# Stores and reloads issued by another engine, late products over all 128 rows, and element-wise work exchanged between ScalarE, VectorE and GpSimd, in a memory attention and two-MLP kernel

## The chip, the cores and the metric

The program runs on one core of a Trainium2 chip. The metric is the device time of one execution in microseconds, median of the runs. On the core TensorE multiplies (in the rows: PE, and PEld for its weight loads), VectorE (DVE), ScalarE (ACT) and GpSimd (POOL) work element-wise, and each engine runs its own instructions strictly in the order written, waiting on semaphores for the others. Transfers run on 16 DMA engines; an instruction on some engine's queue issues them. In the kernel before, all transfers are issued by SyncE (SP, in the rows SPq).

## The reference

```python
# attention between x (8,8,512,64) and state (8,8,32,64), both ways
scores = scale * x @ state.T          # per batch and head: (512, 32)
xread  = softmax(scores) @ state      # every token reads the memory
scores2 = scale * state @ x.T         # (32, 512)
sread  = softmax(scores2) @ x         # every memory slot reads the tokens
t = concat([xread, sread], axis=2)    # 8 x 544 rows of 512
# first MLP
h = t @ w_in                          # 512 -> 2048
y = (relu(h) ** 2) @ w_out            # 2048 -> 512
# second MLP, with a softmax gate and a layer norm
h2 = y @ w2_in                        # 512 -> 1024
s = h2 * softmax(h2)
out = (layer_norm(s) * g_ln) @ w2_out # 1024 -> 512
```

The weights come as 64-bit floats. All products are float32 in quality: an operand is split into a high part, rounded to what TensorE reads in one pass (float32r), and a low part, the rest; a product is three matmuls, high by high, high by low and low by high (`triple`).

## The kernel before, in words

The xread product is folded into the first MLP: since xread is softmax times state, the kernel makes state times w_in once per batch ("sw", 128 rows of head and slot per group of heads, 2048 columns) and multiplies the softmax with it. So a token's hidden layer needs 2 groups of 128 rows in place of 4.

**Prologue.** The 64-bit words of w_in come in 16 units of 128x512 (`fetch_pair`, `fetch_w1in`), are converted by some five VectorE and two ScalarE operations (`convert_parts`), stored for later (`w1i_d`, L213), and multiplied with the state of batches 0 to 3 (`sw_part`). The result goes through ScalarE into a buffer and is stored to HBM (`sw_d`, L287 and L289). Eight units are done ahead of the main loop, together with attention of batch 0.

**Main loop**, 144 steps. An item is a pair (block b, slice f of 128 hidden columns); the first 32 items are the 16 slices of blocks 0 and 1, by halves, and each block after that has 16 items in a row; block 8 holds the sread rows of all batches (256 columns in place of 512). In a step, `hidden` makes 128x512 of the hidden layer in PSUM (6 matmuls, 12 in block 8), ScalarE takes its relu into SBUF (L544), and it is squared by ScalarE (first 16 steps, L546) or by VectorE (after that, L548, r times r). One step later `high` casts it on VectorE (L553) and `low` subtracts on VectorE (L558); two steps later `project` multiplies with w_out into four accumulators (12 matmuls).

Every four steps a chunk of sw is reloaded with four transfers (`load_sw`, L355 for batches 0 to 3), three steps before its first use, and a step later split by `split_sw`: high on ScalarE (L107), low on GpSimd (L108), two tiles of 128x512 each. The buffers of these reloads (tag "stg", four) are those of the weight fetches also.

Between them run, a few pieces a step, attention of the next batch (`attention`), the conversion of the other weights, and in steps 32 to 63 the state-times-w_in products of batches 4 to 7 (`late_part`): 32 times, one product of 128 rows with the high part of the state (L340: rows 0 to 63 are the high part of w_in, rows 64 to 127 its low part, the state stands twice), and one with the low part of the state over rows 0 to 63 (L341).

`sread` (two halves per batch) multiplies softmax and tokens with a stationary tile of 64 columns; the two heads of a pair, i = 0 and 1, go to PSUM rows 0 to 63 and 64 to 127, four token groups t for the one head and then four for the other.

After the loop comes the second MLP, 34 tiles of 128 rows, which the change doesn't touch. Pools set when a buffer is free; the framework orders each engine's queue, in part by its own estimate of durations, so that the order in the trace isn't the program's order line by line.

Of the kernel before, what the change touches and what calls it, by code (L numbers as in the profile page):

```python
# [8 lines left out]
F32 = mybir.dt.float32  # L9
# [3 lines left out]
AF = mybir.ActivationFunctionType  # L13
ALU = mybir.AluOpType
# [6 lines left out]
def memory_attention_relu2_solu(  # L21
# [15 lines left out]
    nc = tc.nc  # L37
    P = 128
    B, H, S, D = x.shape
# [5 lines left out]
    NT = S // P  # L45
    NHP = H // 2
    NQ = H // 4
    NF = F1 // P
    NM = DM // P
    FC = 512  # L50
# [6 lines left out]
    sw_d = [dram.tile([P, B // 4, F1], F32, name=f"sw_d{hp}", tag=f"sw{hp}") for hp in range(NHP)]  # L57
    sw2_d = dram.tile([P, H, F1], F32, name="sw2_d", tag="sw2")

    w1i_d = [dram.tile([P, 2, F1], F32, name=f"w1i_d{k}", tag=f"w1i{k}") for k in range(NM)]  # L60
# [42 lines left out]
    ]  # L103
    sr = srp.tile([P, NHP, NSR], F32, name="sr")

    def split(hi, lo, src, eng=None):
        nc.scalar.activation(out=hi, in_=src, func=AF.Copy)  # L107
        (eng or nc.vector).tensor_tensor(out=lo, in0=src, in1=hi.bitcast(F32), op=ALU.subtract)  # L108

    def triple(ps, pairs, first, last):  # L110

# [6 lines left out]
    def bank(name):  # L118
        return ps_m.tile([P, 512], F32, tag="m", name=name)
# [4 lines left out]
    def u_tile(name):  # L124
        return up_.tile([P, 2, 512], F32R, tag="u", name=name)

    def sw_tile(name):
        return swp.tile([P, 2, 512], F32R, tag="sw", name=name)
# [77 lines left out]
    def convert_w1in(u, st):  # L206

        c, k = divmod(u, NM)

        t = u_tile("w1in")  # L210

        def done():
            nc.sync.dma_start(out=w1i_d[k][:, :, c * FC : (c + 1) * FC], in_=t.bitcast(F32))  # L213
            w1u[u] = t

        flying.append(convert_parts(st, t[:, 0, :], t[:, 1, :], done))
# [55 lines left out]
    def sw_part(u, j):  # L272

        c, hp = divmod(u, NM)
        i = hp % 2
        single = c == 0 and j < 2
        if j % 2 == 0 or single:
            sw_ev[0] = evp.tile([P, 2, 512], F32, tag="ev", name="ev_sw")
        ev = sw_ev[0]
        ps = ps_a.tile([P, 512], F32, tag=f"acc{hp}", name="ps_sw") if u < AHEAD and j < 2 else bank("ps_sw")  # L280
        lh = bd[i][j][:, hp // 2, i].rearrange("p n b -> p (n b)")
        ll = bd[i][j][:, hp // 2, 1 - i].rearrange("p n b -> p (n b)")
        t = w1u[u]
        triple(ps, [(lh, ll, t[:, 0, :], t[:, 1, :])], True, True)
        nc.scalar.activation(out=ev[:, j % 2, :], in_=ps, func=AF.Copy)
        if single:
            nc.sync.dma_start(out=sw_d[hp][:, j, c * FC : (c + 1) * FC], in_=ev[:, j % 2, :])  # L287
        elif j % 2 == 1:
            nc.sync.dma_start(out=sw_d[hp][:, j - 1 : j + 1, c * FC : (c + 1) * FC], in_=ev)  # L289
        if j == 1:  # L290
            w1u.pop(u)

# [37 lines left out]
    def late_part(u, i):  # L330
        c, k = divmod(u, NM)
        if i == 0:
            sw_ev[0] = evp.tile([P, 2, 512], F32, tag="ev", name="ev_sw")
        ev = sw_ev[0]
        ps = bank("ps_sw")
        t = late_w[u]
        h = 2 * k + i
        st = late_st[h // 4]
        o = (h % 4) * P
        nc.tensor.matmul(out=ps, lhsT=st[:, 0, o : o + P], rhs=t[:, i, :], start=True, stop=False)  # L340
        nc.tensor.matmul(out=ps, lhsT=st[:D, 1, o : o + P], rhs=t[:D, i, :], start=False, stop=True)  # L341
        nc.scalar.activation(out=ev[:, i, :], in_=ps, func=AF.Copy)
        if i == 1:
            nc.sync.dma_start(out=sw2_d[:, 2 * k : 2 * k + 2, c * FC : (c + 1) * FC], in_=ev)
            late_w.pop(u)
# [4 lines left out]
    def load_sw(b, c):  # L350
        st = stgp.tile([P, 2, 512], F32, tag="stg", name="stg")
        if b < B // 2:
            for q in range(NQ):
                for i in range(2):
                    nc.sync.dma_start(  # L355
                        out=st[i * 2 * NS : (i + 1) * 2 * NS, q, :],
                        in_=sw_d[2 * q + i][b % 2 :: 2, b // 2, c * FC : (c + 1) * FC],
                    )
        else:
            r = (b - B // 2) * NS  # L360
            for h in range(4):
                nc.sync.dma_start(
                    out=st[h * NS : (h + 1) * NS],
                    in_=sw2_d[r : r + NS, h::4, c * FC : (c + 1) * FC],
                )
        loading[b, c] = st

    def split_sw(b, c):
        st = loading.pop((b, c))
        loaded[b, c] = []  # L370
        for q in range(NQ):
            t = sw_tile("sw")
            split(t[:, 0, :], t[:, 1, :], st[:, q, :], nc.gpsimd)
            loaded[b, c].append(t)

    def load_w1in(c, kk):
# [16 lines left out]
    def attention(b):  # L393
# [82 lines left out]
        def sread(half):  # L476
            if half == 0:
                v["ps_sr"] = bank("ps_sr")
            ps = v["ps_sr"]
            for hp in (2 * half, 2 * half + 1):  # L480
                for i in range(2):
                    h = 2 * hp + i
                    for t in range(NT):
                        nc.tensor.matmul(  # L484
                            out=ps[i * D : (i + 1) * D, hp * NS : (hp + 1) * NS],
                            lhsT=xs_t[b][hp][:, t, i, :],
                            rhs=v["e2", t // 2][:, t % 2, h * NS : (h + 1) * NS],
                            start=(t == 0),
                            stop=(t == NT - 1),
                        )  # L490
            if half == 1:
                nc.scalar.activation(
                    out=sr[:, :, b * NS : (b + 1) * NS],
                    in_=ps[:, : NHP * NS].rearrange("p (h n) -> p h n", n=NS),
                    func=AF.Copy,
                )
# [37 lines left out]
    def hidden(blk, f, w, ah, al, n):  # L534

        c0 = (f % FPC) * P
        ps = ps_h.tile([P, 512], F32, tag="h", name="ps_h")[:, :n]
        pairs = [
            (w[k][:, 0, c0 : c0 + P], w[k][:, 1, c0 : c0 + P], ah[:, k, :], al[:, k, :])
            for k in range(ah.shape[1])  # L540
        ]
        triple(ps, pairs, True, True)
        r = rp.tile([P, 512], F32, tag="r", name="r")[:, :n]
        nc.scalar.activation(out=r, in_=ps, func=AF.Relu)  # L544
        if len(done) < NF:
            nc.scalar.activation(out=r, in_=r, func=AF.Square)  # L546
        else:
            nc.vector.tensor_tensor(out=r, in0=r, in1=r, op=ALU.mult)  # L548
        return r

    def high(b, f, n, r):
        gh = gp.tile([P, 512], F32R, tag="gh", name="gh")[:, :n]
        nc.vector.tensor_copy(out=gh, in_=r)  # L553
        return b, f, n, r, gh

    def low(b, f, n, r, gh):
# [4 lines left out]
    x2_ev = {}  # L561
# [3 lines left out]
    def project(blk, f, n, gh, gl, m):  # L565
        part = NF // 2 if blk < 2 else NF
        if f % part == 0 and m == 0:
            acc[blk] = [ps_a.tile([P, 512], F32, tag=f"acc{i}", name=f"acc{i}")[:, :n] for i in range(NM)]
        wt = w1o[f // 2]
        o = (f % 2) * 512 + m * P  # L570
        triple(acc[blk][m], [(wt[:, 0, o : o + P], wt[:, 1, o : o + P], gh, gl)], f % part == 0, f % part == part - 1)
        if f % part == part - 1:
            if m % 2 == 0:
                x2_ev[0] = evp.tile([P, 2, 512], F32, tag="ev", name="ev_x2")
            ev = x2_ev[0][:, m % 2, :n]
            if f > part:
                nc.vector.tensor_tensor(out=ev, in0=acc[blk][m], in1=x2_part[blk, m // 2][:, m % 2, :], op=ALU.add)
            elif m % 2 == 0:
                nc.scalar.activation(out=ev, in_=acc[blk][m], func=AF.Copy)
            else:  # L580
                nc.vector.tensor_copy(out=ev, in_=acc[blk][m])
            if m % 2 == 1:
                to = x2p_d[blk] if f + 1 < NF else x2_d[blk]
                nc.sync.dma_start(out=to[:, m - 1 : m + 1, :], in_=x2_ev[0][:, :, :n])


    NU = NM * NC1
# [33 lines left out]
    for u in range(NM):  # L621
        begin("i", u)
        for k in range(5):
            advance()
            if k % 2 == 0 and first:
                for piece in first.pop(0):
                    piece()
        if u > 0:
            sw_part(u - 1, 0)
# [159 lines left out]
    done = []  # L789
    for s, (b, f) in enumerate(items):  # L790
# [7 lines left out]
        if g % 5 == 2 and 0 <= g // 5 + 1 < 16:  # L798
            n = g // 5 + 1
# [27 lines left out]
        h = high(*squares.pop(0)) if squares else None  # L827
# [10 lines left out]
        n = S if b < B else NSR  # L838
# [10 lines left out]
        if b < 2 and f in (NF - 4, NF - 3):  # L849
            i = f - NF + 4  # L850
# [43 lines left out]
    for s in range(1, len(tiles) + 2):  # L894
        if s == 1:
            reload_w2(7, 1)
        if s < len(tiles):
            blk, t = tiles[s]
            i = order.index(blk) + 1
# [7 lines left out]
            ps = up(s, blk, t)  # L907
# [36 lines left out]
```

## Time and profile before

| what | value |
|---|---|
| median of 3 runs | 1171.35 us (1170.88 to 1172.41) |
| the profiled execution | 1172.12 us |
| its span in the profile | 1170.3 us |
| TensorE busy | 1124.8 us, 96% of the span |
| VectorE busy | 746.5 us, 64% |
| ScalarE busy | 484.1 us, 41% |
| GpSimd busy | 143.9 us, 12% |

Busy time is the time in which an instruction of the engine is under way; TensorE's instructions overlap, so that a matmul of 0.39 us can start 0.23 us after the one before it. A clock of 1.00 in the rows is TensorE's full 2.4 GHz, 0.5 is 1.2 GHz. "A <- B" in a row of waits says that A stood idle until B was done.

### The profile page before, as it was taken

What the parts mean: (1) busy time and instruction counts of PE and PEld (TensorE: products, weight loads), DVE (VectorE), ACT (ScalarE), POOL (GpSimd) and SP (SyncE); (2) the same over time, 40 slices, a digit from 0 to 9 for tenths busy, and PEclk for the clock granted to TensorE, in tenths of its full rate; (3) what the DMA queues carried; (4) which work ended last, traced back from release to release, by engine and by line L of the source; (5) the groups of instructions that cost most, each with busy time, mean ns of one, the idle gap of its engine ahead of it and who ended that gap; (6) DMA issues with size and microseconds to landing.
All of it is one profiled execution on the core that took longest, in us unless ns stands there. A gap on an engine that the chain in (4) does not pass through costs nothing.

```text
span 1170.3 us, 15242 instructions
## 1 busy us (share of the span) xinstructions
PE 1124.8 (96%) x5672; PEld 914.3 (78%) x5672; DVE 746.5 (64%) x1357; ACT 484.1 (41%) x845; POOL 143.9 (12%) x122
## 2 busy tenths in 40 slices
PE   4787999999999999999999999999999999999997
PEld 2556778777777778888888889988888888888886
DVE  7869999778557569588585554765545454445442
ACT  4657664345445345244342212443434333334232
POOL 0101302132221122222111110000000000000000
PEclk9788999999999999999999999999999999999999
DMA  8775794567565454331310114621101011000000
GB/s 228 242 231 184 267 286 127 161 184 223 180 180 176 128 165 135 89 119 64 91 37 18 73 54 150 229 82 54 64 19 63 18 63 37 28 18 27 19 26 30
DMA packets 93323, 133.66 MB, mean 114 GB/s; under 512 B 45248, under 2 KB 45760, under 8 KB 93248
## 3 DMA queue, kind: packets, MB, share of 16 engines
q1 hardware_dynamic: 93248, 132.68, 36.5%
q8 instruction: 45, 0.74, 0.3%
q14 instruction: 30, 0.25, 0.1%
HBM read 83.37 MB, written 49.28 MB: 113 GB/s over the span
## 4 chain that ended last, share of the span: by engine, by line
PE 84%; DVE 8%; DMA 3%; ACT 2%; issue 1%; POOL 1%; SPq 0%; POOLq 0%; ACTq 0%; DVEq 0%
PE h L703 15%; PE acc L114 10%; PE acc L115 9%; PE acc L116 9%; PE ps_o L754 5%; PE ps_o L752 5%; PE ps_o L753 5%; PE ps_h L114 5%; PE ps_h L116 5%; PE ps_h L115 5%; PE ps_t L742 2%; PE ps_sr L484 2%; PE ps_sw L341 1%; DMA stg<-sw_d 1%; PE ps_x L400 1%
## 5 line engine op out<-in xcount | busy, mean ns | idle before, releaser
L114 PE MATMUL acc<-gh,w1out 128*128 128x512 f32 (+1 forms) x576 | 223.5, 389 | 5.3 <-DVE gh L553 3.9
L115 PE MATMUL acc<-gl,w1out 128*128 128x512 f32 (+1 forms) x576 | 219.4, 381 | 0.0
L116 PE MATMUL acc<-gh,w1out 128*128 128x512 f32 (+1 forms) x576 | 219.2, 381 | 0.0
L548 DVE TENSOR_TENSOR r<-r 128x512 f32<-128x512 f32 (+1 forms) x128 | 99.5, 778 | 119.4 <-ACT r L544 119.3
L108 POOL TENSOR_TENSOR sw<-stg,sw 128x512 fp32r<-128x512 f32 x64 | 101.0, 1590 | 417.1 <-ACT sw L107 245.3
L703 PE MATMUL h<-w,x2h 128*128 128x512 f32 x544 | 148.6, 395 | 0.0
L544 ACT ACTIVATE r<-ps_h 128x512 f32<-128x512 f32 (+1 forms) x144 | 82.3, 572 | 134.9 <-PE ps_h L116 131.2
L114 PEld LDWEIGHTS acc<-gh,w1out 128*128 128x128 f32 x576 | 109.4, 190 | 34.1 <-issue 7.4
L116 PEld LDWEIGHTS acc<-gh,w1out 128*128 128x128 f32 x576 | 109.3, 190 | 20.7
L115 PEld LDWEIGHTS acc<-gl,w1out 128*128 128x128 f32 x576 | 109.5, 190 | 19.8 <-issue 0.5
L703 PEld LDWEIGHTS h<-w,x2h 128*128 128x128 f32 x544 | 99.7, 188 | 18.9
L114 PE MATMUL ps_h<-ah,sw 128*128 128x512 f32 x256 | 107.7, 421 | 0.9 <-ACT ah L107 0.9
L752 PE MATMUL ps_o<-w,lh 128*128 128x512 f32 x272 | 106.1, 390 | 1.0 <-ACT lh L107 1.0
L754 PE MATMUL ps_o<-w,ll 128*128 128x512 f32 x272 | 106.2, 390 | 0.6 <-DVE ll L108 0.6
L753 PE MATMUL ps_o<-w,lh 128*128 128x512 f32 x272 | 105.9, 389 | 0.0
L116 PE MATMUL ps_h<-ah,sw 128*128 128x512 f32 x256 | 101.9, 398 | 1.4 <-POOL sw L108 1.4
L558 DVE TENSOR_TENSOR gl<-r,gh 128x512 fp32r<-128x512 f32 (+1 forms) x144 | 100.5, 698 | 3.4
L115 PE MATMUL ps_h<-al,sw 128*128 128x512 f32 x256 | 101.0, 394 | 0.0
L721 ACT ACTIVATE e<-h,nm 128x1024 f32<-128x1024 f32 x34 | 38.0, 1116 | 143.7 <-DVE nm L718 143.7
L717 DVE TENSOR_REDUCE nm<-h 128x1 f32<-128x1024 f32 x34 | 41.6, 1224 | 86.1 <-PE h L703 86.1
L553 DVE CAST gh<-r 128x512 fp32r<-128x512 f32 (+1 forms) x144 | 80.6, 560 | 9.8 <-ACT r L546 1.9
L703 PE MATMUL h<-w,x2l 128*128 128x512 f32 x272 | 83.8, 389 | 0.0
(131 smaller groups left out, 1715.9 us busy)
## 6 DMA issues: line engine op xcount, KB each, us to landing
stg<-sw_d SPq DMA_DIRECT2D x128, 128.0 KB, 3.0
sw_d<-ev_sw SPq DMA_DIRECT2D x28, 512.0 KB, 4.1
st<-in_moe_w_out_dram SPq DMA_DIRECT2D x24, 512.0 KB, 4.7
xs<-in_x_dram SPq DMA_DIRECT2D x64, 128.0 KB, 3.2
w1i_d<-w1in SPq DMA_DIRECT2D x16, 512.0 KB, 3.9
st<-in_moe_w_in_dram SPq DMA_DIRECT2D x16, 512.0 KB, 5.3
x_d<-ev_x SPq DMA_DIRECT2D x16, 512.0 KB, 2.7
w1in<-w1i_d SPq DMA_DIRECT2D x32, 256.0 KB, 4.7
```

Of the source, the lines that this page charges most:

```text
L108: (eng or nc.vector).tensor_tensor(out=lo, in0=src, in1=hi.bitcast(F32), op=ALU.subtract)
L114: nc.tensor.matmul(out=ps, lhsT=lh, rhs=rh, start=first and i == 0, stop=False)
L115: nc.tensor.matmul(out=ps, lhsT=lh, rhs=rl, start=False, stop=False)
L116: nc.tensor.matmul(out=ps, lhsT=ll, rhs=rh, start=False, stop=last and i == n - 1)
L544: nc.scalar.activation(out=r, in_=ps, func=AF.Relu)
L548: nc.vector.tensor_tensor(out=r, in0=r, in1=r, op=ALU.mult)
L553: nc.vector.tensor_copy(out=gh, in_=r)
L558: nc.vector.tensor_tensor(out=gl, in0=r, in1=gh.bitcast(F32), op=ALU.subtract)
L703: nc.tensor.matmul(out=ps[:, a * 512 : (a + 1) * 512], lhsT=lt[:, k, t * P : (t + 1) * P], rhs=w2[k][:, i, a * 512 : (a + 1) * 512], start ...
L752: nc.tensor.matmul(out=ps, lhsT=a, rhs=wt[:, 0, o : o + 512], start=(k == 0), stop=False)
L753: nc.tensor.matmul(out=ps, lhsT=a, rhs=wt[:, 1, o : o + 512], start=False, stop=False)
L754: nc.tensor.matmul(out=ps, lhsT=bb, rhs=wt[:, 0, o : o + 512], start=False, stop=(k == NK - 1))
```

## The change

It does five things:

- `split_sw`: the low part of sw goes from GpSimd to VectorE.
- `hidden` and `high`: in the first 32 steps ScalarE makes the square twice, once into the float32r tile gh and once in place, one step after the relu, and VectorE's cast goes; from step 32 on VectorE multiplies relu by the PSUM tile itself (r times ps) in place of r times r, and its cast stays.
- `late_part`: the second product runs over all 128 rows; it adds the product of the two low parts.
- `sread`: token groups outside, heads inside, so that the two heads alternate.
- The stores of w1i_d, of sw_d and of the first half of x2p_d, and the reloads of sw for batches 0 to 3 are issued by GpSimd's queue in place of SyncE's.

```diff
-    def split(hi, lo, src, eng=None):
+    def split(hi, lo, src):
         nc.scalar.activation(out=hi, in_=src, func=AF.Copy)
-        (eng or nc.vector).tensor_tensor(out=lo, in0=src, in1=hi.bitcast(F32), op=ALU.subtract)
+        nc.vector.tensor_tensor(out=lo, in0=src, in1=hi.bitcast(F32), op=ALU.subtract)
...
-            nc.sync.dma_start(out=w1i_d[k][:, :, c * FC : (c + 1) * FC], in_=t.bitcast(F32))
+            nc.gpsimd.dma_start(out=w1i_d[k][:, :, c * FC : (c + 1) * FC], in_=t.bitcast(F32))
...
-            nc.sync.dma_start(out=sw_d[hp][:, j, c * FC : (c + 1) * FC], in_=ev[:, j % 2, :])
+            nc.gpsimd.dma_start(out=sw_d[hp][:, j, c * FC : (c + 1) * FC], in_=ev[:, j % 2, :])
...
-            nc.sync.dma_start(out=sw_d[hp][:, j - 1 : j + 1, c * FC : (c + 1) * FC], in_=ev)
+            nc.gpsimd.dma_start(out=sw_d[hp][:, j - 1 : j + 1, c * FC : (c + 1) * FC], in_=ev)
...
-        nc.tensor.matmul(out=ps, lhsT=st[:D, 1, o : o + P], rhs=t[:D, i, :], start=False, stop=True)
+        nc.tensor.matmul(out=ps, lhsT=st[:, 1, o : o + P], rhs=t[:, i, :], start=False, stop=True)
...
-                    nc.sync.dma_start(
+                    nc.gpsimd.dma_start(
                         out=st[i * 2 * NS : (i + 1) * 2 * NS, q, :],
                         in_=sw_d[2 * q + i][b % 2 :: 2, b // 2, c * FC : (c + 1) * FC],
...
-            split(t[:, 0, :], t[:, 1, :], st[:, q, :], nc.gpsimd)
+            split(t[:, 0, :], t[:, 1, :], st[:, q, :])
...
-                for i in range(2):
-                    h = 2 * hp + i
-                    for t in range(NT):
+                for t in range(NT):
+                    for i in range(2):
+                        h = 2 * hp + i
...
         nc.scalar.activation(out=r, in_=ps, func=AF.Relu)
-        if len(done) < NF:
+        if len(done) >= 2 * NF:
+            nc.vector.tensor_tensor(out=r, in0=r, in1=ps, op=ALU.mult)
+        return r
+
+    def high(b, f, n, r):
+        gh = gp.tile([P, 512], F32R, tag="gh", name="gh")[:, :n]
+        if b < 2:
+            nc.scalar.activation(out=gh, in_=r, func=AF.Square)
             nc.scalar.activation(out=r, in_=r, func=AF.Square)
         else:
-            nc.vector.tensor_tensor(out=r, in0=r, in1=r, op=ALU.mult)
-        return r
-
-    def high(b, f, n, r):
-        gh = gp.tile([P, 512], F32R, tag="gh", name="gh")[:, :n]
-        nc.vector.tensor_copy(out=gh, in_=r)
+            nc.vector.tensor_copy(out=gh, in_=r)
...
-                nc.sync.dma_start(out=to[:, m - 1 : m + 1, :], in_=x2_ev[0][:, :, :n])
+                (nc.gpsimd if f + 1 < NF else nc.sync).dma_start(out=to[:, m - 1 : m + 1, :], in_=x2_ev[0][:, :, :n])
```

## Rows read from the trace of the kernel before

**Rows 1.** The page: the engines' busy time, share of the span and instructions

```profile
PE 1124.8 (96%) x5672; PEld 914.3 (78%) x5672; DVE 746.5 (64%) x1357; ACT 484.1 (41%) x845; POOL 143.9 (12%) x122
```

**Rows 2.** Busy time by stretch: PE, PEld, DVE, ACT, POOL, clock, DMA share, GB/s

```profile
0.00:60.00 60.00, 36.88 (x187) 25.73 (x188) 46.93 (x97) 34.72 (x65) 4.13 (x10) 0.83 0.81 239
60.00:82.00 22.00, 16.93 (x65) 11.18 (x64) 15.56 (x30) 13.01 (x24) 0.00 (x0) 0.86 0.71 213
82.00:126.00 44.00, 37.24 (x202) 28.67 (x201) 40.23 (x85) 28.16 (x51) 10.09 (x4) 0.88 0.62 210
126.00:206.00 80.00, 78.28 (x353) 63.49 (x352) 75.64 (x142) 47.50 (x85) 16.49 (x10) 1.00 0.74 219
206.00:247.00 41.00, 39.04 (x234) 31.90 (x233) 29.27 (x42) 13.31 (x25) 9.80 (x6) 1.00 0.62 167
247.00:424.00 177.00, 177.00 (x861) 132.57 (x860) 114.09 (x191) 79.44 (x138) 34.19 (x23) 1.00 0.60 177
424.00:760.00 336.00, 335.67 (x1860) 284.70 (x1859) 225.74 (x382) 119.01 (x205) 50.53 (x35) 1.00 0.31 100
```

**Rows 3.** TensorE's matmuls in order of time around one late part: start, duration

```profile
247.91 0.39 PE L340 MATMUL ps_sw<-w1in,st_t 128*128 128x512 f32 x1
248.23 0.50 PE L341 MATMUL ps_sw<-w1in,st_t 64*128 64x512 f32 x1
248.66 0.50 PE L114 MATMUL acc<-gh,w1out 128*128 128x512 f32 x1
248.99 0.39 PE L115 MATMUL acc<-gl,w1out 128*128 128x512 f32 x1
249.22 0.39 PE L116 MATMUL acc<-gh,w1out 128*128 128x512 f32 x1
```

**Rows 4.** Weight loads of one half of sread, counted from 233.90 to three ends

```profile
233.90:234.17 0.27, 0.23 (x4) 1.00 1.04 266
233.90:234.95 1.05, 1.01 (x28) 1.00 0.97 220
233.90:235.26 1.36, 1.32 (x32) 1.00 0.91 211
```

**Rows 5.** Groups by line: busy us, mean ns, idle before and its releaser

```profile
L108 POOL TENSOR_TENSOR sw<-stg,sw 128x512 fp32r<-128x512 f32 x64 | 101.0, 1590 | 417.1 <-ACT sw L107 245.3 <-PE ps_h L116 82.9 <-DMA stg<-sw_d 58.3
...
L108 DVE TENSOR_TENSOR ll<-ps_t,lh 128x512 fp32r<-128x512 f32 x68 | 43.6, 682 | 12.8 <-ACT lh L107 12.8
...
L546 ACT ACTIVATE r<-r 128x512 f32<-128x512 f32 x16 | 10.1, 630 | 0.1
...
L548 DVE TENSOR_TENSOR r<-r 128x512 f32<-128x512 f32 x112 | 92.8, 829 | 108.7 <-ACT r L544 108.6
L553 DVE CAST gh<-r 128x512 fp32r<-128x512 f32 x128 | 75.9, 593 | 8.7 <-ACT r L546 1.9 <-PE acc L116 1.1
```

**Rows 6.** TensorE's waits: for whom, us in total, times, longest

```profile
PE ps_h L116 <- POOL sw L108: 1.4, 3, 0.7
PE ps_st L313 <- DVE st_t L108: 2.0, 1, 2.0
```

**Rows 7.** SyncE's queue and TensorE's start of attention 1: start, issue time

```profile
27.73 0.33 SPq L287 DMA_DIRECT2D sw_d<-ev_sw  x1
...
54.30 0.60 SPq L390 DMA_DIRECT2D xs<-in_x_dram  x1
...
63.41 0.51 SPq L289 DMA_DIRECT2D sw_d<-ev_sw  x1
63.98 0.61 SPq L390 DMA_DIRECT2D xs<-in_x_dram  x1
...
66.70 5.17 SPq L390 DMA_DIRECT2D xs<-in_x_dram  x6
...
69.10 0.63 PE L400 MATMUL ps_x<-ident,xs 128*128 128x128 f32 x4 [0.86 <-issue]
```

**Rows 8.** GpSimd in order of time, the two lows of one chunk of sw

```profile
113.92 7.52 POOL L108 TENSOR_TENSOR sw<-stg,sw 128x512 fp32r<-128x512 f32 x2 [22.08 <-DMA stg<-sw_d]
```

More of the change, by code (lines that the diff above doesn't have):

```diff
@@ L544, in hidden @@
         nc.scalar.activation(out=r, in_=ps, func=AF.Relu)
-        if len(done) < NF:
-            nc.scalar.activation(out=r, in_=r, func=AF.Square)
-        else:
-            nc.vector.tensor_tensor(out=r, in0=r, in1=r, op=ALU.mult)
+        if len(done) >= 2 * NF:
+            nc.vector.tensor_tensor(out=r, in0=r, in1=ps, op=ALU.mult)
         return r
@@ L552, in high @@
         gh = gp.tile([P, 512], F32R, tag="gh", name="gh")[:, :n]
-        nc.vector.tensor_copy(out=gh, in_=r)
+        if b < 2:
+            nc.scalar.activation(out=gh, in_=r, func=AF.Square)
+            nc.scalar.activation(out=r, in_=r, func=AF.Square)
+        else:
+            nc.vector.tensor_copy(out=gh, in_=r)
         return b, f, n, r, gh
```

## The prediction

> **What bounds the kernel now.** I read the page first: TensorE is busy 96% of the span, no other engine that computes more than 64% [rows 1]. So the end is set by how fast TensorE gets through its queue, and an edit elsewhere pays only where TensorE waits. The table by stretch shows where that is [rows 2]. From 247 on it doesn't wait: 177.00 of 177 us busy, then 335.67 of 336. Up to 247 it stands idle 23.1 us in the first 60 (start-up), 5.1 in 60 to 82, 6.8 in 82 to 126, 1.7 in 126 to 206 and 2.0 in 206 to 247. In those stretches VectorE is the fullest: 40.23 of 44 and 75.64 of 80 us. The clock is full from 126 on; it is 0.86 in 60 to 82 and 0.88 in 82 to 126, which with two levels means 6.2 and 10.6 us at 1.2 GHz.
>
> A busy TensorE isn't one at its best pace, so I read its matmuls in order of time next, as starts and not as durations. Two ordinary matmuls of 512 columns start 0.23 us apart (248.99 to 249.22) [rows 3]. Two places of this kernel are slower than that while they count as busy, and the change touches both.
>
> **The late product, 12.5 us.** Around the product over 64 rows the starts are 0.32, 0.43 and 0.33 us apart: from the 128-row product to it, from it to the next, and once more after that [rows 3]. From 247.91 to 249.22 there are four steps in 1.31 us where ordinary ones take 0.92. The 128-row product at 247.91 has the same columns and none of this before it, so I put the 0.39 us down to the change of the row count there and back. All 32 lie in the stretch where TensorE never waits [rows 2], so all of it is on the path: 32 x 0.39 = 12.5 us. More rows of the same columns cost nothing by the same row, which excludes a loss; the other bound is nothing gained, if the delay has another cause.
>
> **sread with the heads alternating, 4 us.** One half is 32 weight loads. The first four start within 0.23 us, 57 ns apart; the next 24 need 0.78 us, 32 ns apart; the last four are slow again [rows 4]. The two heads of a pair write to different halves of PSUM's rows and use different columns of the array. I read this as each head's loads going 57 ns apart, with the other head's running between them where a run of eight meets the next; at both ends a head is alone. If they alternate all along, 31 steps of 28.5 ns take 0.88 us in place of 1.18 (the 1.32 less one load's 0.14, which is what is left after the last start). That is 0.30 us for each of 16 halves, 4.8 us; the first four belong to batches 0 and 1, in the prologue and the first steps, where time saved can be lost again, so I take 4. Nearest row for the other bound: if every change of head cost one more half of the 57 ns, 16 changes would make it 0.15 us longer a half, plus 2.4 in all.
>
> **VectorE and ScalarE.** In the first 32 steps VectorE loses 32 casts of 0.593 and 16 squares of 0.829 and gets 16 lows, for which I take its own row of the same shape from PSUM, 0.682: minus 19.0, minus 13.3, plus 10.9, together minus 21.4 us, of which steps 0 to 15 have 9.5 less 5.5 [rows 5]. ScalarE gets two squares where it had one or none: 48 x 0.630 = 30.2 us, 0.94 a step. It has 47.50 of 80 us in 126 to 206 [rows 2]; a step is 18 matmuls, 4.1 us at least, so there are at most 19 steps and it comes to 66 of 80 at most. What hides it is that a slice of the hidden layer is projected two steps after it is made; without that cover each step would be late by up to one square, 20 us in 32 steps. Removing the waits on VectorE and on GpSimd's lows takes away 2.0 and 1.4 us of TensorE's idle time [rows 6]; of the 3.7 us between 126 and 247 I take 3, with bounds 0 and 3.7.
>
> After step 32 VectorE gets 48 lows, 32.7 us, and r times ps in place of r times r for 96 steps of 512 columns. The nearest row with one operand in PSUM is again 0.682 against 0.829, minus 14.1. The rest, 19 us or 0.2 a step, goes into an engine that is busy 225.74 of 336 us there [rows 2]: nothing. The product also holds the hidden tile in PSUM until it is done, 0.68 us and its queue longer; there are two such tiles and the next use is two steps away, some 8 us, so nothing again, and 0.68 us a step if VectorE were ever that far behind.
>
> **The queues, 3 us.** 104 transfers leave SyncE's queue: 16 stores of w1i, 20 of sw, 4 of x2p, 64 reloads. What stood behind them shows in SyncE's queue: one load of x for attention 1 at 54.30, the next at 63.98, directly behind a store of sw at 63.41 which waits for ScalarE's eviction, and six more from 66.70 on [rows 7]. TensorE starts attention 1 at 69.10 after 0.86 us of idle time, and attention's short steps are where the 5.1 us of 60 to 82 are lost. With the stores elsewhere these loads wait for their own buffers only, which sread of batch 0 gives back in the prologue. Also, the two lows of the third chunk took GpSimd 7.52 us [rows 8]; on VectorE two take 1.36 and their place in its queue. I put the gain at half of the 11.8 us idle between 60 and 126, 6 us. More than 14, all of the idle time and a little clock, I exclude.
>
> Against it stands the price of a transfer issued by GpSimd, of which the trace has none. Lower bound: what SyncE pays, 0.5 to 0.9 us an issue [rows 7]. Upper bound: GpSimd's slowest work beside a full VectorE, 3.76 us (half of 7.52). An issue reads and writes no tile, so I take a value near the lower one, 1 us over SyncE's. A chunk's path is one store, four reloads in a row and the split; three chunks are early enough for TensorE to feel it, and I put down 1 us each: plus 3, with bounds 0 and, at 3.76 an issue and two chunks fully exposed, plus 14 (net plus 8). In steps 32 to 63 32 reloads on GpSimd stand beside the multiplication of the w2 conversion; three steps, over 12 us, lie before each use: nothing.
>
> The Trainium skill, page DMA: Bandwidth & Descriptors, section Latency and other measured facts, gives about 1 us to the first byte from GpSimd's queue against 0.6 from SyncE's; no row here shows it, and by that alone the plus 3 would be some plus 1.
>
> **Sum.** The profiled execution took 1172.12 us, span 1170.3 and 1.8 around it. Minus 12.5, minus 4, minus 3, minus 6, plus 3: 1149.6. It is 0.8 over the median of the runs, so the forecast is 1149.
>
> **Rivals.**
> - *The early chunks eat the gain of the start.* The queue's net is plus 8 in place of minus 3: 1160. For it: VectorE is at 95%, so the lows wait their turn there too, and the reloads are on the way to the hidden layer. Against it: TensorE has attention and other slices to work on.
> - *GpSimd becomes the bound, and the kernel gets slower.* 72 of the 104 transfers fall before step 32, between the first store at 27.73 [rows 7] and the first late product at 247.91 [rows 3], 220 us. At 3.76 us each they need 271, plus 51; less the 16.5 of the late products and sread, 1206. It decides from (220 + 16) / 72 = 3.3 us an issue. For it: GpSimd needed 7.52 us for two operations of a mean of 1.59 [rows 5, 8] while VectorE was full. Against it: VectorE becomes emptier by 21.4 us, and an issue is not a tile operation.
>   The Trainium skill, page SBUF — State Buffer, section SBUF: two separate sides, names this as the trap of transfers issued from GpSimd: their descriptors can't be written while VectorE holds the port that the two share. By that rule this rival is what happens; the 7.52 us agrees that VectorE can hold GpSimd up, and that an issue suffers likewise no row shows.
> - *The delay around the late product isn't the row count:* 1149 + 12.5 = 1161. Against it: the product over 128 rows beside it has none.
> - *The start gets whole:* the queue's net is minus 14, and the clock no longer falls between 60 and 126: 1138. For it: the waits there follow on each other. Against it: VectorE has little room, 40.23 of 44 us.
>
> **Chances.** Forecast 0.56, early chunks 0.20, GpSimd the bound 0.10, the delay stays 0.06, the start whole 0.08. The bounds added up without GpSimd as the bound give 1136 and 1169; leaving out the third rival and the tails, the range is 1138 to 1164. About 0.2% is what a measurement of this kernel can tell from no change. Slower by more: 0.09, nearly all of the second rival; within: 0.03, from the edge between that and the first; faster: 0.88. The likeliest case's own range is 1144 to 1155.
>
> **What would show it.** The late product starts 0.23 us after the one before it and so do the two after: right, else the 12.5 is wrong. The 32 loads of a half start over 0.9 us: right; over 1.2 or more: wrong. The loads of x for attention 1 follow each other directly, and TensorE's idle time from 60 to 126 is near 9 us: right. GpSimd's issues over 2 us each, or TensorE waiting for reloaded sw in every chunk: the slow rival. Most of all the forecast fails if the price of GpSimd's issues is far from 1 us above SyncE's.

## The result, and the profile after

The changed kernel takes 1159.65 us, median of 4 runs (1157.97 to 1160.17), against 1171.88 us before beside them: a ratio of 0.9894, 95% interval 0.9877 to 0.9911, or 12 us faster. The forecast was 1149, range 1138 to 1164. The time is within the range, outside the likeliest case's own (1144 to 1155), and where the first rival stood (1160). The profiled execution took 1159.73 us, span 1158.0.

The page's line of engines, after, to set beside [rows 1]:

```profile
PE 1108.7 (96%) x5672; PEld 915.1 (79%) x5672; DVE 716.9 (62%) x1373; ACT 511.5 (44%) x893; POOL 102.4 (9%) x162
```

The table by stretch, columns as in [rows 2]:

```profile
0.00:60.00 60.00, 33.33 (x113) 23.40 (x114) 42.03 (x87) 30.59 (x57) 11.60 (x26) 0.83 0.74 228
60.00:82.00 22.00, 17.39 (x130) 12.06 (x128) 17.32 (x34) 18.03 (x33) 5.71 (x9) 0.99 0.83 263
82.00:126.00 44.00, 38.36 (x207) 30.48 (x208) 41.81 (x90) 32.85 (x60) 8.44 (x15) 0.85 0.64 212
126.00:206.00 80.00, 76.60 (x342) 62.67 (x341) 62.50 (x121) 58.49 (x106) 20.03 (x33) 0.98 0.64 212
206.00:247.00 41.00, 41.00 (x246) 33.66 (x245) 22.50 (x40) 25.11 (x44) 8.89 (x14) 1.00 0.64 182
247.00:424.00 177.00, 174.30 (x910) 141.89 (x909) 120.30 (x219) 83.50 (x146) 19.84 (x28) 1.00 0.61 186
```

VectorE is far emptier in 126 to 206 (62.50 us against 75.64), and TensorE nevertheless is idle there 3.4 us where it was 1.7. The idle time of the first 60 us grew from 23.1 to 26.7. Where the 12 us come from shows in the starts of the relu (L544) of single steps, read from the traces; the last two rows are experiments of the next section:

| kernel | step 0 | step 16 | step 32 | step 143 | steps 32 to 143 | span |
|---|---|---|---|---|---|---|
| before | 57.1 | 161.9 | 242.7 | 757.8 | 515.1 | 1170.3 |
| after | 55.1 | 168.4 | 243.1 | 745.7 | 502.6 | 1158.0 |
| late product and sread alone | 56.3 | 164.8 | 244.7 | 744.1 | 499.4 | 1156.7 |
| all moves, transfers on SyncE | 50.9 | 154.7 | 230.9 | 730.1 | 499.2 | 1142.8 |

Up to step 32 the change gained nothing, 243.1 against 242.7; all of the gain lies behind it.

The late product, TensorE's matmuls of after in order of time (start, duration):

```profile
248.14 0.39 PE L116 MATMUL acc<-gh,w1out 128*128 128x512 f32 x1
248.36 0.39 PE L340 MATMUL ps_sw<-w1in,st_t 128*128 128x512 f32 x1
248.59 0.39 PE L341 MATMUL ps_sw<-w1in,st_t 128*128 128x512 f32 x1
248.82 0.39 PE L114 MATMUL acc<-gh,w1out 128*128 128x512 f32 x1
249.04 0.39 PE L115 MATMUL acc<-gl,w1out 128*128 128x512 f32 x1
```

All starts are 0.22 or 0.23 us apart, where [rows 3] had 0.32, 0.43 and 0.33. One half of sread, the weight loads of after in a stretch that holds exactly the 32 of it (length, busy time and count, clock, DMA share, GB/s):

```profile
234.90:236.10 1.20, 1.01 (x32) 1.00 0.39 87
```

1.01 us in place of the 1.32 of [rows 4]. The groups of the moved operations, columns as in [rows 5]:

```profile
L546 DVE TENSOR_TENSOR r<-r,ps_h 128x512 f32<-128x512 f32 x96 | 65.8, 685 | 84.8 <-ACT r L544 84.6
...
L108 DVE TENSOR_TENSOR sw<-stg,sw 128x512 fp32r<-128x512 f32 x64 | 45.8, 715 | 30.3 <-ACT sw L107 30.2
...
L555 DVE CAST gh<-r 128x512 fp32r<-128x512 f32 x96 | 42.4, 441 | 4.1
...
L553 ACT ACTIVATE r<-r 128x512 f32<-128x512 f32 x32 | 20.1, 628 | 0.5
L552 ACT ACTIVATE gh<-r 128x512 fp32r<-128x512 f32 x32 | 20.0, 628 | 0.6
```

The operations cost what they were put down at (0.685 and 0.715 us for the 0.682 taken). The surprise is the cast that did not move: 0.441 us, where it took 0.593.

Now the start. GpSimd's queue in after, in order of time (start, length of the issue, and in brackets how long GpSimd stood before it and for whom):

```profile
21.25 0.56 POOL L287 DMA_DIRECT2D sw_d<-ev_sw  x1 [0.98 <-ACT ev_sw L285]
21.86 0.53 POOL L355 DMA_DIRECT2D stg<-sw_d  x1
28.78 0.52 POOL L355 DMA_DIRECT2D stg<-sw_d  x1 [6.39 <-DMA sw_d<-ev_sw]
29.30 0.73 POOL L213 DMA_DIRECT2D w1i_d<-w1in  x1
29.91 0.67 POOL L287 DMA_DIRECT2D sw_d<-ev_sw  x1
35.44 0.54 POOL L355 DMA_DIRECT2D stg<-sw_d  x1 [4.86 <-DMA sw_d<-ev_sw]
```

An issue takes 0.5 to 0.7 us here. What takes long is the standing: GpSimd waits 6.39 us for a store to land before it can issue the reload of the same data, and the next store of sw (29.91), whose eviction ended on ScalarE at 26.03, stands behind that wait. ScalarE's queue of after, in the same stretch:

```profile
25.43 0.60 ACT L285 ACTIVATE ev_sw<-ps_sw 128x512 f32<-128x512 f32 x1 [0.28 <-PE ps_sw L116]
26.75 0.59 ACT L418 ACTIVATE st<-ps_s 64x512 f32<-64x512 f32 x1 [0.73 <-PE ps_s L414]
27.37 0.72 ACT L183 ACTIVATE cz<-cz,rebias 128x512 int32<-128x512 int32 x1
33.12 0.63 ACT L107 ACTIVATE sw<-stg 128x512 fp32r<-128x512 f32 x1 [5.04 <-DMA stg<-sw_d]
33.66 0.70 ACT L183 ACTIVATE cz<-cz,rebias 128x512 int32<-128x512 int32 x1
34.27 0.71 ACT L460 ACTIVATE st<-st,cm 128x512 f32<-128x512 f32 x1
...
34.97 1.13 ACT L441 ACTIVATE e<-e 128x512 f32<-128x512 f32 x2
```

The copy of the split waits 5.04 us for its reload, and behind it in ScalarE's order stand the two softmaxes of batch 0, that of sread (L460) and that of xread (L441), which need no reload; what L441 reads was ready on VectorE at 31.31. The waits of ScalarE and then of TensorE in the first 260 us of after (us in all, times, longest):

```profile
ACT sw L107 <- DMA stg<-sw_d: 15.7, 8, 5.0
```

```profile
PE ps_a L507 <- DVE e L450: 9.2, 1, 9.2
PE acc L115 <- DVE gl L560: 4.3, 1, 4.3
PE acc L114 <- ACT ev_x L581: 3.4, 1, 3.4
```

The 9.2 us of TensorE are the end of that chain: copy, softmax (L441), VectorE's normalisation (L450). Before, ScalarE waited 2.3 us in all for reloads and TensorE 5.3 us for that normalisation, so the chain costs some 3.9 us here. The row on ev_x has the same cause at 138: the eviction of an accumulator stands behind a copy whose reload was issued at 128.51 and landed at 136.2.

### The profile page after: what moved, and what is told of

The parts are those of the page before. It is cut to its first block, busy times and chain, and to the rows that moved or that the text cites. A ratio compares the mean times of both kernels' runs of the same rounds, so it can differ in the third digit from the quotient of the medians.

```text
span 1158.0 us, 15282 instructions
## 1 busy us (share of the span) xinstructions
PE 1108.7 (96%) x5672; PEld 915.1 (79%) x5672; DVE 716.9 (62%) x1373; ACT 511.5 (44%) x893; POOL 102.4 (9%) x162
## 4 chain that ended last, share of the span: by engine, by line
PE 84%; DVE 4%; DMA 3%; ACT 1%; issue 1%; POOL 0%; POOLq 0%; ACTq 0%; DVEq 0%
PE h L705 15%; PE acc L116 10%; PE acc L115 10%; PE acc L114 10%; PE ps_h L114 5%; PE ps_o L756 5%; PE ps_o L754 5%; PE ps_o L755 5%; PE ps_h L116 5%; PE ps_h L115 5%; PE ps_t L744 2%; PE ps_sr L484 1%; DMA st<-in_moe_w_in_dram 1%; PE ps_x L400 1%; DMA stg<-sw_d 1%
## 5 line engine op out<-in xcount | busy, mean ns | idle before, releaser
L114 PE MATMUL acc<-gh,w1out 128*128 128x512 f32 (+1 forms) x576 | 217.9, 380 | 4.3 <-ACT ev_x L581 3.4
L116 PE MATMUL acc<-gh,w1out 128*128 128x512 f32 (+1 forms) x576 | 220.1, 382 | 0.0
L544 ACT ACTIVATE r<-ps_h 128x512 f32<-128x512 f32 (+1 forms) x144 | 82.5, 573 | 139.0 <-PE ps_h L116 134.9
L546 DVE TENSOR_TENSOR r<-r,ps_h 128x512 f32<-128x512 f32 (+1 forms) x112 | 72.5, 647 | 96.6 <-ACT r L544 96.4
L560 DVE TENSOR_TENSOR gl<-r,gh 128x512 fp32r<-128x512 f32 (+1 forms) x144 | 96.2, 668 | 14.5 <-ACT r L553 11.3
L733 POOL TENSOR_TENSOR var<-var,mhalf 128x1 f32<-128x1 f32 x34 | 18.6, 548 | 589.6 <-DVE var L732 589.6
L107 ACT ACTIVATE sw<-stg 128x512 fp32r<-128x512 f32 x64 | 40.2, 627 | 59.5 <-PE ps_h L116 43.2
```

Source lines behind the costliest of these rows:

```text
L114: nc.tensor.matmul(out=ps, lhsT=lh, rhs=rh, start=first and i == 0, stop=False)
L116: nc.tensor.matmul(out=ps, lhsT=ll, rhs=rh, start=False, stop=last and i == n - 1)
L546: nc.vector.tensor_tensor(out=r, in0=r, in1=ps, op=ALU.mult)
L560: nc.vector.tensor_tensor(out=gl, in0=r, in1=gh.bitcast(F32), op=ALU.subtract)
```

## The experiments

All ratios are to the kernel before on the same chip, with 95% intervals.

**1. Late product alone, and with sread, on the kernel before.**

```diff
-        nc.tensor.matmul(out=ps, lhsT=st[:D, 1, o : o + P], rhs=t[:D, i, :], start=False, stop=True)
+        nc.tensor.matmul(out=ps, lhsT=st[:, 1, o : o + P], rhs=t[:, i, :], start=False, stop=True)
...
-                for i in range(2):
-                    h = 2 * hp + i
-                    for t in range(NT):
+                for t in range(NT):
+                    for i in range(2):
+                        h = 2 * hp + i
```

> The kernel before with the late product over 128 rows alone. Both theories of the missing gain (ScalarE's fuller queue in the first 150 us; the slower transfers of GpSimd's queue) expect the term in full, 32 x 0.39 = 12.5 us: 1159.4, with the starts around L341 0.23 us apart. If instead time saved there is lost again elsewhere, 1163 to 1168.

> The kernel before with the late product over 128 rows and the heads alternating in sread, nothing else. Both theories: 12.5 + 4.8, at least 16.5 us, 1154 to 1155, some 5 us under the changed kernel, with the first 32 steps as they were before. If the two terms don't hold by themselves, 1159 or more, and the rest of the change costs nothing.

Measured: the late product alone 1159.46 us (0.9888, 0.9872 to 0.9903), 12.4 us under the 1171.81 beside it; with sread 1156.28 (0.987, 0.9848 to 0.9892), another 3.2, a little over the 1154 to 1155 expected. By the times alone these 3.2 are not clear of noise; the traces show them in steps 32 to 143, which the first run shortens by 12.4 us and the second by another 3.3. These two parts alone are no slower than the whole change. So the rest of it, together, gave nothing or cost a little.

**2. All of the change but the queue, and the queue alone.** The first is the changed kernel with `nc.sync` again at the five places of the diff that issue by `nc.gpsimd`; the second is the kernel before with these five edits and nothing else.

> The changed kernel with all stores and reloads back on SyncE's queue. If GpSimd's transfers are what the change loses, about 1154, and TensorE's first long wait (9.2 us on VectorE's e) falls back to 5.3. If it is ScalarE's order and its added squares, 1158 to 1161, with waits on ScalarE's evictions near 135 us still there.

> The kernel before with the stores and reloads issued by GpSimd alone. If its transfers are what the change loses, 1176 to 1178, and the time is lost before 60 us. If they cost nothing, 1170 to 1173; if freeing SyncE's queue is a gain by itself, as forecast, 1166 to 1169.

Measured: without the queue's move 1145.14 us (0.9773, 0.9759 to 0.9787), which beats both kernels; with the queue's move alone 1189.41 (1.0144, 1.0126 to 1.0163). Both lie further out than the theory of the transfers had them (1154 and 1176 to 1178). So moving the transfers costs 14.5 us on the changed kernel and 17.6 on the one before, and the exchange between the engines gains 11.1 (1156.28 to 1145.14). Two stretches of the version on SyncE, to set beside the table of after:

```profile
82.00:126.00 44.00, 38.94 (x219) 30.44 (x220) 40.98 (x90) 35.04 (x65) 0.00 (x0) 0.92 0.63 210
126.00:206.00 80.00, 79.93 (x366) 65.51 (x365) 65.74 (x126) 60.82 (x110) 0.00 (x0) 1.00 0.74 225
```

Up to 247 TensorE is idle 33.1 us there in all, in after 40.3. The granted clock has a part too: 0.92 and 1.00 in these stretches, 0.85 and 0.98 in after. After the wait of 3.40 us on ev_x, for instance, TensorE's matmuls in after start 0.42 to 0.43 us apart from 139.8 to 142.8, and 0.23 again behind that.

**3. Half the transfers.** The changed kernel with only its stores on GpSimd (first), and with only its reloads there (second).

```diff
-                    nc.gpsimd.dma_start(
+                    nc.sync.dma_start(
                         out=st[i * 2 * NS : (i + 1) * 2 * NS, q, :],
```

> The changed kernel with the 64 reloads of sw back on SyncE's queue, the stores still on GpSimd's. If the reloads' path (waiting in GpSimd's queue, then landing 1.4 us later) is what costs the 14.5 us, 1146 to 1149. If the stores' later landing does it (what they store from comes free later, and the reload waits for them), 1154 to 1159.

> The changed kernel with all stores back on SyncE's queue, the reloads still on GpSimd's. Reload theory: 1154 to 1159, with ScalarE still waiting some 15 us for reloads in the first 260 us. Store theory: 1146 to 1149.

Measured: 1152.5 (0.9832, 0.9814 to 0.985) and 1151.41 (0.9827, 0.9813 to 0.9841), 7.4 and 6.3 us over the version on SyncE. Neither half alone is the cause, against both theories as they stood. TensorE's wait for the first normalisation is back at 5.2 and 5.3 us in both, so what they cost lies behind it. A later experiment shows that these two also differ in something else than their transfers.

**4. The exchange taken apart**, on the version that issues from SyncE: once with the squares and casts as before (first), once with sw's lows back on GpSimd (second).

```diff
-            split(t[:, 0, :], t[:, 1, :], st[:, q, :])
+            split(t[:, 0, :], t[:, 1, :], st[:, q, :], nc.gpsimd)
```

> The kernel with all on SyncE's queue (1145), with the squares and casts as before the change; the lows of sw stay on VectorE. It parts the 11 us between that kernel and the one with the late product and sread alone (1156.3). If GpSimd's lows were the cost (they hold VectorE up and are held up), 1146 to 1149; if the 32 casts and 16 squares taken from VectorE are the gain, 1153 to 1157.

> The same kernel of 1145 with the lows of sw on GpSimd again, squares as in the changed kernel. If GpSimd's lows were the cost, 1153 to 1157; if the squares and casts are the gain, 1146 to 1149. Both near 1150: each gives half.

Measured: 1146.83 (0.9784, 0.9769 to 0.9799) and 1152.36 (0.9844, 0.9824 to 0.9865), the second just under the 1153 to 1157 expected of the lows. With the late products and sread alone at 1156.28, the lows gain 9.5 us (to 1146.83) or 7.2 (1152.36 to 1145.14), squares and casts 3.9 or 1.7. The lows' gain is clear of noise; that of squares and casts is not, since the intervals of the ratios overlap in both pairs. What the lows do to VectorE shows in two groups each of the kernel with late product and sread alone, whose lows run on GpSimd, and of the one with old squares, whose lows run on VectorE; these instructions are the same in both:

```profile
L548 DVE TENSOR_TENSOR r<-r 128x512 f32<-128x512 f32 x112 | 92.5, 826 | 98.5 <-ACT r L544 98.4
L553 DVE CAST gh<-r 128x512 fp32r<-128x512 f32 x128 | 76.0, 593 | 8.1 <-ACT r L546 1.4 <-PE acc L116 1.1
```

```profile
L548 DVE TENSOR_TENSOR r<-r 128x512 f32<-128x512 f32 x112 | 78.9, 704 | 86.0 <-ACT r L544 86.0
L553 DVE CAST gh<-r 128x512 fp32r<-128x512 f32 x128 | 55.8, 437 | 5.0 <-DVE r L548 0.5 <-PE acc L116 0.4
```

With GpSimd's lows VectorE's operations take longer in the mean: 0.826 for 0.704 us, 0.593 for 0.437. The first trace shows where: 28 of the 128 casts run while a GpSimd tile operation is under way and take 1.20 us in the mean, the other 100 take 0.42; of the 112 products 31 take 1.19, the rest 0.69. The product that reads PSUM (r times ps) isn't slowed: in the second kernel of this experiment it takes 0.685 us both beside GpSimd's work (24 of 96) and without it. The two groups shown give VectorE back 33.8 us, against the 45.7 us that the 64 lows cost it. And on GpSimd the lows themselves stretch, in order of time, in the kernel with late product and sread alone; of the pair, the first takes 8.69 us:

```profile
86.16 1.26 POOL L108 TENSOR_TENSOR sw<-stg,sw 128x512 fp32r<-128x512 f32 x1 [36.24 <-ACT sw L107]
...
113.72 9.93 POOL L108 TENSOR_TENSOR sw<-stg,sw 128x512 fp32r<-128x512 f32 x2 [21.99 <-DMA stg<-sw_d]
```

**5. Only the stores that nobody soon waits for** (w1i_d) on GpSimd, the rest on SyncE.

```diff
-            nc.sync.dma_start(out=w1i_d[k][:, :, c * FC : (c + 1) * FC], in_=t.bitcast(F32))
+            nc.gpsimd.dma_start(out=w1i_d[k][:, :, c * FC : (c + 1) * FC], in_=t.bitcast(F32))
```

> The kernel with every move of the change but all stores and reloads on SyncE (1145.1 us), and only the 16 stores of w1in's parts (w1i_d) issued by GpSimd. Nothing waits for what these stores write until long after, but the tile they are read from is needed again. If only transfers cost that somebody soon waits for (sw's stores and reloads), this is 1144 to 1147, or a little under 1144 if SyncE's queue gains by losing them. If every transfer on GpSimd costs by its late landing, because the tile is given back later, 16 of the 36 stores would take some 3 of the 7.4 us that the stores cost: 1147 to 1150.

Measured: 1142.96 (0.9762, 0.9746 to 0.9779). They cost nothing on the whole; a gain over the 0.9773 of the version on SyncE isn't shown.

**6. The split a step later**, in the changed kernel (first) and in the version on SyncE (second).

```diff
-            elif s % FPC == 2:
+            elif s % FPC == 3:
                 split_sw(*nxt)
```

> The changed kernel (1159.65 us), with the split of reloaded sw issued one step later: ScalarE's copies then stand one step, over 4 us, further behind the reloads in its queue. Theory: half of the queue's price is ScalarE standing in order behind reloads that haven't landed (15.7 us of its time in the first 260 us, longest wait 5.0). Then that wait falls under 6 us and the time to 1150 to 1155. Rival: the price is the reloads' landing itself, which TensorE's hidden layer needs, in whatever place the copies stand: then 1158 to 1163, since a later split also leaves the hidden layer less time.

> The same later split in the kernel with all stores and reloads on SyncE (1145.1 us). There ScalarE waits only 1.2 us for reloads in the first 260 us, so the theory gives nothing to gain: 1145 to 1148, the 0 to 3 being the hidden layer's shorter lead. That shows what of the other run's difference is the split's place alone.

Measured: 1159.49 (0.9904, 0.9886 to 0.9922) and 1142.98 (0.9764, 0.9748 to 0.978): nothing in either. But the first is no test of its theory. ScalarE waits 14.3 us for reloads as before the edit, and comparing the two traces, 294 of its 307 instructions of the first 260 us stand in the same order: the framework put the copies back to nearly the same place. That led to the next question: how far does the order itself differ when the issuer changes? Between the changed kernel and the version on SyncE, of those 307 only 230 stand in the same order (the longest common sequence by operation, tiles and shape; on TensorE 1012 of 1088, on VectorE 295 of 383); between the kernel before and the one with late product and sread alone it is 257 of 259. A transfer moved to another queue made the framework write another order for each of these engines. Another order need not be a slower one: the kernel of experiment 5 has 249 of ScalarE's 319 in the order of the version on SyncE, and its time.

**7. The same transfers in the other order.** The changed kernel with all 104 transfers on GpSimd, each engine's instructions chained, without waits, in the order of the version on SyncE. ORDER is that order, NO_WAIT the framework's dependency without a semaphore.

```diff
+def follow(tc, nc):
+    traced = list(nc.cur_bb.bb.instructions)
+    last = {}
+    for i, d in enumerate(json.loads(zlib.decompress(base64.b64decode(ORDER)))):
+        ins = traced[i + d]
+        eng = str(ins.engine)
+        if eng in last:
+            tc.add_manual_dep(ins, last[eng], NO_WAIT, reason="follow")
+        last[eng] = ins.name
...
         memory_attention_relu2_solu(tc, *args)
+        follow(tc, nc)
```

> The changed kernel, its 104 transfers on GpSimd, but every engine's instructions chained in the order of the version that issues them from SyncE (1145.1 us): the framework orders the queues by its own estimate, and with the transfers on GpSimd it wrote another order for ScalarE, VectorE and TensorE in the first 260 us. First theory, the transfers themselves are what costs (a reload or store lands later, and what waits for it stands in an engine's order): the order changes little, 1155 to 1162, and ScalarE still waits 8 us or more for reloads. Rival, the order written for GpSimd's transfers is what costs: then this run comes near the SyncE version, 1144 to 1150, although the transfers land as late as before. Between 1150 and 1155 both have a share.

Measured: 1147.94 us (1146.38 to 1153.2; ratio 0.981, 0.9778 to 0.9842). Its trace has the order that it was given: of the first 260 us all 315 instructions of ScalarE, all 1136 of TensorE and all 395 of VectorE stand as in the version on SyncE. By medians it is 2.8 us over that version and 11.7 under the changed kernel; by ratios, times the 1171.35 of before, 4.3 and 9.8. The rival holds: of the 14.5 us, some 3 to 4 are the transfers and some 10 to 12 the order written for them, GpSimd's own order included. The runs scatter, four from 1146.4 to 1148.7 and two at 1152.8 and 1153.2, and the intervals of the ratios leave 0 to 8 us for the transfers and 6 to 14 for the order: the second is clear of zero, the first barely.

The transfers are no faster here. The same 64 reloads (L355) of three kernels, of the version on SyncE, of after and of this kernel:

```profile
DMA to landing us min/median/max: 2.6/4.5/7.5
```

```profile
DMA to landing us min/median/max: 2.5/4.2/8.1
```

```profile
DMA to landing us min/median/max: 2.5/4.7/8.1
```

So a reload doesn't land later for being issued by GpSimd; the 1.4 us in the first expectation of experiment 3 came from setting these 64 beside SyncE's 64 reloads of later steps, which land after 2.8 us. The stores do land later: those of sw of 256 KB (L287) after 2.9, 4.6 and 3.8 us in the same three kernels, those of 512 KB (L289) after 3.4, 5.9 and 5.6, those of w1i (L213) after 4.5, 5.2 and 5.1 (medians). A reload is issued only when its store has landed.

What the order does shows in ScalarE's queue of this kernel, in the stretch shown of after:

```profile
27.99 0.60 ACT L285 ACTIVATE ev_sw<-ps_sw 128x512 f32<-128x512 f32 x1
28.48 0.71 ACT L460 ACTIVATE st<-st,cm 128x512 f32<-128x512 f32 x1
...
29.89 1.23 ACT L441 ACTIVATE e<-e 128x512 f32<-128x512 f32 x2 [0.61 <-DVE e L438]
32.54 0.72 ACT L467 ACTIVATE st<-st,cs 128x512 f32<-128x512 f32 x1 [1.42 <-DVE sm L448]
34.44 0.63 ACT L107 ACTIVATE sw<-stg 128x512 fp32r<-128x512 f32 x1 [1.18 <-DMA stg<-sw_d]
```

The softmaxes run at 28.48 and 29.89 in place of 34.27 and 34.97, and the copy behind them, at 34.44, waits 1.18 us in place of 5.04. ScalarE's and TensorE's waits there, first 260 us:

```profile
ACT sw L107 <- DMA stg<-sw_d: 6.7, 6, 2.3
```

```profile
PE ps_a L507 <- DVE e L450: 5.3, 1, 5.3
PE acc L115 <- DVE gl L560: 3.1, 1, 3.1
```

Its granted clock in two stretches is that of the version on SyncE:

```profile
82.00:126.00 44.00, 39.21 (x218) 30.39 (x219) 41.11 (x90) 34.73 (x65) 9.01 (x15) 0.92 0.59 203
126.00:206.00 80.00, 78.05 (x351) 62.70 (x350) 65.50 (x124) 59.82 (x108) 18.65 (x32) 1.00 0.70 215
```

TensorE is idle 34.6 us up to 247, and step 32 begins at 234.4, 8.7 us before the 243.1 of after. The kernel with the queue's move alone shows the other side: its copy stands at 33.17, waits 5.16 us and has the softmaxes behind it, at 34.32 and 35.02, as in after.

## Why the prediction was partly right, point by point

That 1159.65 lies in the range owes something to luck. Two terms of the sum held. The other two missed on opposite sides: the exchange gave 8 us more than was put down, and the queues cost 14.5 us where a gain of 3 was expected. With the two as forecast the time would have been 1149; with the exchange as measured and the queues as forecast it would lie near 1141, and it is the queues' cost that brought it back up into the range.

**The late product: right.** 32 x 0.39 = 12.5 us were forecast; the starts are 0.22 to 0.23 us apart and the product alone gave 12.4. The rival in which the delay stays is out.

**sread: right.** 0.88 us for 32 loads and 4 us in all were forecast; the first load to the last take 0.876 us (235.013 to 235.889), and the part gave 3.2 by medians and 3.3 in steps 32 to 143 of the traces, which hold 10 of the 16 halves. The picture of it was a little off: the loads go in pairs, 6 or 7 ns within a pair and 48 to 52 to the next, not evenly every 28.5.

Both terms sit where TensorE never waits, and steps 32 to 143 became 515.1 less 499.4 = 15.7 us shorter with these two parts alone. In the changed kernel it is 12.5; 2.7 us of idle time are new in 247 to 424.

**VectorE and ScalarE: right in sign, too small.** The term was 3 us with bounds 0 and 3.7; the exchange measured 11.1. The step that failed is that it counted VectorE's time as a sum of durations that don't depend on what GpSimd does, and the gain as the waits seen in 126 to 247 alone. The traces show the operations that stayed getting shorter with GpSimd's lows gone, and most of the 11 us come with the lows. The 14.1 us of VectorE's time put down for r times ps were mostly of this kind too: with the lows on VectorE r times r takes 0.704 us in place of 0.826, near the 0.685 of r times ps. How much of it is work and how much the order that goes with it isn't told apart: experiments 2 and 4 have an order of their own each (of ScalarE's 259 instructions in the first 260 us of the kernel with late product and sread alone, 217 stand in the same order once the lows are on VectorE too). That ScalarE's squares, 0.628 us each, lie in cover held on the whole: VectorE's low now waits 11.3 us in all for the second square (L553), but TensorE for that low only once, the 4.3 us shown, where before it waited once 3.9 for the cast.

**The queues: wrong in sign.** Minus 6 and plus 3 were put down, net minus 3; measured plus 14.5. Three things are in it.
- *The price of the transfers, plus 3: about right in size, by another way.* With the order held, GpSimd's issuing costs some 3 to 4 us net, 0 to 8 by the intervals. But an issue is not 1 us longer: the 16 reload issues in 20 to 140 us take 0.52 to 1.09 us, median 0.55, and took SyncE 0.45 to 1.08, median 0.59; the stores' take a median of 0.56 to 0.70 us, in the version on SyncE 0.33 to 0.55. What is longer is the stores' way to landing, by 0.6 to 2.5 us in the medians above, and GpSimd stands in order between a store and its reload as SyncE did. That this is what makes the 3 to 4 us was not tested. Two bounds of this term were misread. GpSimd's slowest work was not 3.76 us, the half of a pair: of the two lows behind the 7.52 in [rows 8] the first took 5.84 and the second 1.71. And plus 14 at 3.76 an issue is one chunk fully exposed, five issues of some 3 us more than SyncE's, not two.
- *The gain at the start, minus 6: not there.* As forecast, the loads of x stand together in SyncE's queue (eight from 61.98 on), but with the order held the kernel that frees SyncE isn't the faster one, and moving the w1i stores alone gave a change that isn't told from none. TensorE's idle time in 60 to 126 went from 11.8 to 10.3 us, not to 9, and the first 60 us lost 3.5 more. So nothing here shows that the load behind the store in [rows 7] set the pace.
- *The order, 10 to 12 us: not in the sum at all.* The sum let every instruction keep its place. The rewritten order puts copies before work that could have run, so a late reload holds up a softmax that has nothing to do with it. Two of TensorE's waits followed above are part of it: 3.9 us of the 9.2 at the start, and the 3.4 on ev_x. The rest of the 10 to 12 was not followed wait by wait.

**The rivals.** *The early chunks eat the gain* named the place and nearly the time, 1160, with chance 0.20. But it blames the price of issues, and with the same issues in another order the time was 1147.94; the time agreed because an exchange worth 8 us more than forecast made up for most of the order's cost. *GpSimd becomes the bound* is out: it decides from 3.3 us an issue, and GpSimd is busy 102.4 us in all. *The start gets whole*, 1138, came nearest in the versions with most or all transfers on SyncE, 1143 to 1145, and not through the queue. The 1169 given as the bounds added up leaves out the late product's own bound, nothing gained: with 12.5 for it, 6.4 for sread, 3 for the exchange and 11 for the queues, 1149 becomes some 1182.

The rule quoted for the second rival, of the Trainium skill, page SBUF — State Buffer, section SBUF: two separate sides, speaks of descriptors that can't be written while VectorE holds the port. The traces don't show it for the reloads: the longest issue of a reload took 1.09 us, though VectorE was busy 41.81 of 44 us in 82 to 126, and the 64 landed no later than from SyncE. The stores did land later; whether by this rule or by something else, no run here tells apart.

**Open.** What in the framework's estimate makes it write this order was not read from any trace. Which engine's order costs how much was not taken apart. That the order also explains the 17.6 us of the queue alone, or the halves of experiment 3, was not run.

## What to carry to other kernels

Where a framework writes the queues from its own estimates, an edit that only changes who issues a transfer is an edit to the order of every engine: compare the orders first, and run the new transfers in the old order, before any time is laid to the hardware. An operation that waits for a transfer should stand behind work that doesn't: what cost time here was less the copy's own lateness than that of the softmax queued behind it. Landing times are to be compared for the same transfers in the same stretch, not between early and late steps. And the price of a tile operation on GpSimd is to be looked for on VectorE too, in operations of the same shape that become slower.

## What the runs showed of the hardware that was not expected

- VectorE's cast of 128x512 took 1.20 us in the mean while a GpSimd tile operation was under way and 0.42 otherwise, r times r 1.19 and 0.69; the product with an operand in PSUM took 0.685 either way. A low on GpSimd took 8.69 us once where another took 1.26.
- The same 64 reloads of 128 KB landed after a median of 4.2 and 4.7 us when GpSimd issued them (after, and experiment 7) and of 4.2 and 4.5 when SyncE did (before, and the version on SyncE). The same stores landed 0.6 to 2.5 us later from GpSimd than in the version on SyncE.
- A reload's issue costs GpSimd no more than SyncE (0.55 against 0.59 us), a store's 0.1 to 0.2 us more. The 16 stores of w1i alone cost no time there, with the order that was written for them: 1142.96 us with them moved, 1145.14 without.
